# Block-sparse attention and a bilinear FFN on one core: the attention outputs of three batches are turned by a DMA transpose, and the queries lie twice in DRAM

## The chip, the cores and the metric

The kernel runs on one core of a Trainium2 chip. The metric is the time of one execution on the device in microseconds. Before the change three runs gave 824.2, 828.27 and 829.44 us, so the median is 828.27 us.

## The reference

Four batches of eight heads with 768 positions and a head size of 64 go through block-sparse attention (blocks of 32; each block of queries sees its neighbours, the first and the last block, and three sampled ones; the first and the last block see everything). The outputs of all heads of a position make a row x of 512, and 3072 such rows go through (x·w_a)·(x·w_b) and then w_out.

```python
scores = scale * np.matmul(q, k.transpose(0, 1, 3, 2))
mask = np.abs(blk_i - blk_j) <= window
mask = mask | (blk_i == 0) | (blk_j == 0) | (blk_i == n_blocks - 1) | (blk_j == n_blocks - 1)
# ... and the sampled blocks
attn = np.exp(scores - max) / (sum + 1e-09)
x = np.matmul(attn, v)            # (B, H, S, D) -> (B * S, H * D) = (3072, 512)
out = ((x @ w_a) * (x @ w_b)) @ w_out
```

## The kernel before, in words

Values are float32. The kernel takes most operands as a pair of f16 numbers (high and low part), so that a product is the sum of two or three f16 products. The first batch (b = 0) is the exception: its scores and values are multiplied in float32.

**Units.** One block of 32 queries of one batch, all heads, is a unit: 24 units a batch, 96 in all. For a unit TensorE (PE) makes the scores (`s`, line 932, lines 923 and 1068 with it), VectorE (DVE) their maximum, ScalarE (ACT) the exponentials `sm`. ACT and DVE split these in f16 pairs `hl`, a DMA transpose on SyncE's queue (SP) turns them to `pt` (line 1135; line 1239 for the dense first and last unit of a batch), and PE multiplies `pt` with gathered values `VG` into `av` (line 991). SP also issues the gathers of `VG` (lines 706 to 719). They go into two buffers.

**Outputs.** Two units share a bank `av` of PSUM. `output` takes each pair of units: for b > 0 ACT copies one half (`xs`, line 1294), DVE adds the other half (1295) and divides (1296); PE turns the two 128x128 float32 tiles of `xs` with the unit matrix (line 1301, into the same bank), and ACT and DVE split what it wrote in high and low part in `xT` (1312 and 1313). The bank comes free after that. There are 12 pairs in a batch, so 36 in batches two to four.

**FFN.** Eight units (four pairs) make a chunk of 256 rows; there are 12 chunks, and three buffers `xT`. `first_products` makes 12 groups of 24 matmuls for a chunk (line 1350, 128x256 each, `xT` as the moving operand, 3456 in all); `inner` multiplies the two halves; `second_products` makes 12 groups of six for w_out (lines 1432 to 1434), after `split` has made pairs `gh` of the gates.

**Queries of batches two to four.** Half a chunk's queries are loaded on 64 partitions by ACT's queue (line 746); ACT takes the bound (776) and the high part (782), DVE the low part (784); then `turn_queries` copies each part to the other 64 partitions with a DMA on SP (line 822): two for a half, 36 in all. 64 partitions are not enough, because a key's high and low part stand on top of each other on 128 partitions.

**Keys and values.** For each batch four tiles of keys and four of values pass a ring of three buffers `ks`. The bound of a tile of values (`va`, line 581) uses a buffer of that ring for output that nobody reads.

**Order.** The program is written out by a planner. Each flow (a generator) asks for the next instruction with a cost; the planner gives each engine its instructions in an order by estimated times and ranks, and every engine then runs its own queue in that order. A wait at the head of a queue holds up all behind it. `LATE_…` constants are delays that the planner adds to an estimate; they make no instruction wait.

## Time and profile before

| | |
|---|---|
| median of three runs | 828.27 us |
| the profiled execution's own time | 832.1 us |
| its span, first to last instruction | 830.3 us |
| PE busy | 757.6 us, 91% |
| weight loads on PE | 533.0 us, 64% |
| DVE busy | 525.1 us, 63% |
| ACT busy | 485.3 us, 58% |
| POOL (GpSimd) busy | 172.7 us, 21% |
| mean granted clock of PE | 0.971 |
| packets on SP's queue (q1), share of 16 DMA engines | 48.6% |

The durations are those of one execution, whose own time is 3.8 us over the median of the runs. PE is busy in nearly all slices from 150 us to the end; the first 150 us, with the loads and the first batch, leave it idle more often. The durations of matmuls have modelled ends, so for PE the distance from one start to the next says more than the length.

### The profile page before, as it was taken

The page shows a single profiled execution, that of the slowest core. Times are in us where ns is not written, and L with a number is a line of the kernel's source. Part 1 is how long each engine was busy: PE and PEld are TensorE (multiplying, and loading weights), DVE is VectorE, ACT ScalarE, POOL GpSimd, SP SyncE. Part 2 cuts the span into 40 slices and gives each one's busy share as a digit, 9 for nine tenths or more (in the row PEclk, how much of TensorE's full clock was granted, in tenths as well). Part 3 has the DMA queues.
Part 4 walks back from the last instruction along what each step waited for, and adds up shares of the span by engine and source line. Part 5 has one row for each costly group of instructions (what it writes and reads, how often), then busy time and mean ns, then how long its engine had stood idle before and what let it go on. Part 6 is the DMA issues. An engine that isn't in the chain of part 4 may idle for free.

```text
span 830.3 us, 26115 instructions
## 1 busy us (share of the span) xinstructions
PE 757.6 (91%) x10128; PEld 533.0 (64%) x10128; DVE 525.1 (63%) x1495; ACT 485.3 (58%) x1189; POOL 172.7 (21%) x430
## 2 busy tenths in 40 slices
PE   3759699999997989899799999999999999999998
PEld 1426477764586468748558848848758668768853
DVE  3679998866746755686657676766566666532232
ACT  3456777886646554775645666766456655533333
POOL 4405321012123321130223221301123212000000
PEclk9859999999999899999999999999999999999999
DMA  7788877477577688869777779769776665440001
GB/s 226 224 280 252 240 198 213 147 206 176 135 149 144 139 213 148 178 167 185 175 162 137 151 181 228 174 162 188 148 151 148 128 124 128 111 116 2 1 1 52
DMA packets 171803, 130.50 MB, mean 157 GB/s; under 512 B 116894, under 2 KB 138527, under 8 KB 171679
## 3 DMA queue, kind: packets, MB, share of 16 engines
q1 hardware_dynamic: 156844, 86.29, 48.6%
q10 hardware_dynamic: 14832, 42.54, 17.0%
q8 instruction: 80, 1.31, 0.7%
q14 instruction: 47, 0.36, 0.1%
HBM read 86.31 MB, written 11.01 MB: 117 GB/s over the span
## 4 chain that ended last, share of the span: by engine, by line
PE 72%; DMA 10%; DVE 8%; ACT 5%; SPq 2%; issue 2%; ACTq 0%; POOL 0%; POOLq 0%; DVEq 0%
PE ab L1350 40%; PE o L1432 6%; PE o L1434 6%; PE o L1433 6%; PE av L991 5%; PE s L932 4%; DMA VG<-in_v_dram 3%; DMA keysT<-ks 2%; PE av L1301 2%; PE s L923 2%; DMA VG<-vd 2%; ACT gh L1402 1%; DVE gh L1403 1%; PE tp L1039 1%; DMA QZ<-in_q_dram 1%
## 5 line engine op out<-in xcount | busy, mean ns | idle before, releaser
L1350 PE MATMUL ab<-xT,wab 128*128 128x256 f16 x3456 | 396.0, 274 | 2.7 <-DVE g L1368 2.7
L1350 PEld LDWEIGHTS <-wab 128*128 128x128 f16 x3456 | 334.1, 98 | 58.1 <-issue 17.1
L1368 DVE TENSOR_TENSOR g<-g,ab 128x256 f32<-128x256 f32 x144 | 60.4, 419 | 145.8 <-ACT g L1365 141.9
L1365 ACT ACTIVATE g<-ab,f 128x256 f32<-128x256 f32 x144 | 67.9, 471 | 110.5 <-PE ab L1350 106.8
L1402 ACT ACTIVATE gh<-g,scale 128x256 f16<-128x256 f32 x144 | 70.5, 504 | 79.4 <-PE o L1434 74.0
L1403 DVE SCALAR_TENSOR_TENSOR gh<-g,scale,gh 128x256 f16<-128x256 f32 x144 | 68.8, 490 | 75.1 <-ACT gh L1402 73.9
L1432 PE MATMUL o<-wo,gh 128*128 128x512 f16 x288 | 110.4, 383 | 0.1
L1434 PE MATMUL o<-wo,gh 128*128 128x512 f16 x288 | 110.2, 383 | 0.0
L1433 PE MATMUL o<-wo,gh 128*128 128x512 f16 x288 | 110.2, 383 | 0.0
L653 POOL COPY KG<-keysT 128x384 int32<-128x384 int32 (+1 forms) x86 | 47.8, 556 | 278.8 <-PE s L932 237.8
L662 POOL COPY KG<-keysT 128x128 int32 (+1 forms) x264 | 92.6, 388 | 51.8 <-POOL KG L653 32.3
L1095 ACT ACTIVATE sm<-s,low,cq 128x256 f32<-128x256 f32 x132 | 73.7, 560 | 47.4 <-DVE low L1089 38.8
L991 PE MATMUL av<-VG,pt 128*32 128x128 f16 (+2 forms) x3584 | 68.4, 217 | 27.2 <-DMA VG<-in_v_dram 13.0
L421 POOL PARTITION_ALL_REDUCE power<-bound x58 | 22.7, 391 | 296.0 <-DVE bound L1382 126.9
L958 DVE SCALAR_TENSOR_TENSOR hl<-sm,hl 128x256 f16<-128x256 f32 (+1 forms) x156 | 69.6, 450 | 1.7
L1083 DVE TENSOR_REDUCE low<-s 128x2 f32<-128x512 f32 x88 | 60.2, 684 | 13.9 <-PE s L923 9.0
L991 PEld LDWEIGHTS <-pt 128*32 128x32 f16 x2688 | 33.0, 97 | 34.8 <-issue 22.5
L1434 PEld LDWEIGHTS <-gh 128*128 128x128 f16 x288 | 28.4, 99 | 34.6 <-issue 0.8
L1432 PEld LDWEIGHTS <-gh 128*128 128x128 f16 x288 | 28.2, 98 | 34.8 <-issue 4.3
L1433 PEld LDWEIGHTS <-gh 128*128 128x128 f16 x288 | 28.3, 98 | 28.6 <-issue 0.6
L1372 ACT ACTIVATE junk<-g 128x1024 f16<-128x1024 f32 x36 | 38.0, 1055 | 8.5 <-DVE g L1368 8.5
L954 DVE TENSOR_SCALAR hl<-sm 128x256 f16<-128x256 f32 (+1 forms) x125 | 39.3, 317 | 5.5 <-ACT sm L1095 5.2
(122 smaller groups left out, 876.0 us busy)
## 6 DMA issues: line engine op xcount, KB each, us to landing
VG<-vd SPq DMA_DIRECT2D x210, 64.0 KB, 2.2
VG<-vd SPq DMA_DIRECT2D x66, 192.0 KB, 3.2
VG<-vd SPq DMA_DIRECT2D x24, 384.0 KB, 3.8
out_dram<-ou ACTq DMA_DIRECT2D x24, 256.0 KB, 3.5
VG<-in_v_dram SPq DMA_DIRECT2D x74, 64.0 KB, 3.7
stage<-in_v_dram ACTq DMA_DIRECT2D x12, 384.0 KB, 6.7
q<-in_q_dram ACTq DMA_DIRECT2D x18, 256.0 KB, 4.6
vd<-vs SPq DMA_DIRECT2D x12, 384.0 KB, 4.2
```

The source lines that it names most:

```text
L662: nc.gpsimd.tensor_copy(to[:, :, (5 + r) * w : (6 + r) * w], of[:, :, bass.ds(at, w)])
L958: t = yield dve(221 + n * 1.03, lambda: nc.vector.scalar_tensor_tensor(lo, sm, over, hi, ALU.mult, ALU.subtract))
L991: mm(both[hs, :, i % 2, hq] if two else av[hs, i % 2, hq], pt[:, y, hs], of if two or b == 0 else of[:, 0], start=(i % 2 == 0 and hq == 0 ...
L1095: t = yield act(750, lambda hq=hq: nc.scalar.activation(sm[:, hq], ps[:, hq], AF.Exp, bias=low[:, at, hq, 0:1], scale=factor_of(b, cc, hq) ...
L1350: mm(ab[:, i, :], wab[:, f, i, part, kt, :], xc[:, kt, a, :], start=(i == 0 and kt == 0 and part + a == 0), stop=(kt == KT - 1 and a == 1) ...
L1365: yield act(460, lambda: nc.scalar.activation(g, ab[:, 0, :], AF.Copy, scale=f1[:, f : f + 1]))
L1368: t = yield dve(415, lambda: nc.vector.tensor_mul(g, g, ab[:, 1, :]))
L1402: yield act(400, lambda: nc.scalar.activation(gh[:, 0], g, AF.Copy, scale=s))
L1403: t = yield dve(480, lambda: nc.vector.scalar_tensor_tensor(gh[:, 1], g, s, gh[:, 0], ALU.mult, ALU.subtract))
L1432: mm(po, gh[:, 0, js], wo[:, f, 0], start=(f == 0), stop=False)
L1433: mm(po, gh[:, 0, js], wo[:, f, 1], start=False, stop=False)
L1434: mm(po, gh[:, 1, js], wo[:, f, 0], start=False, stop=(f == NF - 1))
```

## The change

The outputs of batches two to four are no longer turned by PE. After line 1296 ACT makes the high part `xo` of `xs`, DVE the low part, and one DMA transpose on SP turns the four 128x128 f16 tiles (high and low of two tiles) straight into `xT`. The bank `av` is free in the plan after the addition. So that a transpose writes one piece, `xT` is laid out by pairs: pair, high or low, tile, four groups of heads, 32 positions. The products of line 1350 read 256 columns of it as eight runs of 32. The first batch keeps PE's transposes, into the new layout.

The queries are laid out twice, one below the other, in DRAM; a load brings both copies to 128 partitions, ACT and DVE split on all of them, and the copies of `turn_queries` are gone. The ring `ks` has two buffers; `va` writes to `junk`, a tile that only ACT writes.

```diff
-KS_BUFS = 3
+KS_BUFS = 2
+XO_BUFS = 2
+LATE_XO = 1000
+LATE_XT = 2500
...
-    xT = [kvp.tile([P, KT, 2, CH], F16, name=f"xT{i}") for i in range(X_BUFS)]
+    xT = [kvp.tile([P, PER // 2, 2, 2, KT, BLK], F16, name=f"xT{i}") for i in range(X_BUFS)]
...
-        done = yield from take("ks", KS_BUFS)
-        spare = work.tile([P, 2 * NT, P], F16, tag="ks", name=f"va{b}_{g}", bufs=KS_BUFS)
         end = yield act(1020, lambda: nc.scalar.activation(
-            spare[:, :NT], t, AF.Abs,
-            accum_out=bound_v[:, b * NG + g : b * NG + g + 1],
-        ))
-        done.fire(end)
+            junk.rearrange("p f c -> p (f c)")[:, : NT * P].rearrange("p (t x) -> p t x", t=NT),
+            t, AF.Abs, accum_out=bound_v[:, b * NG + g : b * NG + g + 1],
+        ))
...
-            end = yield load_way(700, lambda t=t, half=half: nc.scalar.dma_start(
-                t[:D], q[b, c, :, half * NG : (half + 1) * NG]
+            end = yield load_way(2000, lambda t=t, half=half: nc.scalar.dma_start(
+                t, q[b, c, :, half * NG : (half + 1) * NG]
...
-    def turn_queries(cc, half, a):
-
-        heads = slice(half * NG, (half + 1) * NG)
-        yield SPARE
-        end = yield sp(650, 400, lambda: nc.sync.dma_start(
-            QT[cc][D:, 1 - a, heads], QT[cc][:D, a, heads]
-        ))
-        q_ready[cc].fire(end)
...
-        to = xT[p % X_BUFS][:, :, :, i % PER * BLK : (i % PER + 2) * BLK]
+        to = xT[p % X_BUFS][:, i % PER // 2]
...
             yield act(470, lambda: nc.scalar.copy(xs, sums[:, 1]))
-            yield dve(418, lambda: nc.vector.tensor_add(xs, xs, sums[:, 0]))
+            t = yield dve(418, lambda: nc.vector.tensor_add(xs, xs, sums[:, 0]))
+            read.fire(t + LATE_AV)
             yield dve(430, lambda: nc.vector.tensor_mul(xs, xs, over))
-        ps = bank[:, 1].rearrange("p (g i x) -> p g i x", g=NG, i=2)
+            gone = yield from take("xo", XO_BUFS)
+            xo = work.tile([P, 2, 2, P], F16, tag="xo", name=f"xo{b}_{i}", bufs=XO_BUFS)
+            flat = xs.rearrange("p i a d -> p i (a d)")
+            yield act(400, lambda: nc.scalar.copy(xo[:, 0], flat))
+            t = yield dve(420, lambda: nc.vector.tensor_sub(xo[:, 1], flat, xo[:, 0]))
+            held.fire(t)
+            t = yield sp(900, 760, lambda: nc.sync.dma_start_transpose(
+                to.rearrange("p a x k q -> p (a x) (k q)"), xo.rearrange("p a i c -> p (a i c)")
+            ))
+            gone.fire(t + LATE_XO)
+            x_ready[cc].fire(t + LATE_XT)
+            x_ready[cc].fire(t + LATE_XT)
+            return
...
                                 mm(
-                                    ab[:, i, :], wab[:, f, i, part, kt, :], xc[:, kt, a, :],
+                                    ab[:, i, :].rearrange("p (j x q) -> p j x q", j=PER // 2, x=2),
+                                    wab[:, f, i, part, kt, :], xc[:, :, a, :, kt, :],
...
+        a = np.concatenate([a, a], axis=2)
```

Three places show how the instructions move. In the names below a number behind a tile counts pieces or allocations.

PE before, at the fourth pair of the second batch (`av_6`, `xs_6`), between two groups of second products (`o`, `gh`):

```order
L1433 MATMUL o_1_4589<-wo,gh_0_4557 128x512
L1434 LDWEIGHTS gh_0_4557
L1434 MATMUL o_1_4589<-wo,gh_0_4557 128x512
L1301 MATMUL av_6_4329<-eye,xs_6_4553 128x4x32 x2
L1432 LDWEIGHTS gh_1_4558
L1432 MATMUL o_0_4588<-wo,gh_1_4558 128x512
```

In the changed kernel no row of line 1301 is left on PE behind the first batch, 12 instead of 48 pairs in all; the groups stand next to each other there.

ACT before, at the same pair, from the copy of `xs_6` to the high part in `xT`:

```order
L1294 COPY xs_6_4553<-av_6_4329 128x256
L951 ACTIVATE hl_4517<-sm_4504 128x256
L1402 ACTIVATE gh_3_4624<-g_0_3241,scale 128x256
L776 ACTIVATE QT_4198,bound<-q_1_4506 64x1024
L1095 ACTIVATE sm_4636,den<-s_4554,low,cq 128x256
L1402 ACTIVATE gh_4_4647<-g_4_3694,scale 128x256
L1312 ACTIVATE xT_86<-av_6_4329 128x4x64
```

ACT in the changed kernel, at the same pair: `xo_6` is the high part of `xs_6`, and `ab_11` the last group of first products of the chunk before this pair's own:

```order
L749 DMA q_1_4442<-in_q_dram 128x1024
L1286 COPY xs_6_4486<-av_6_4281 128x256
L1087 ACTIVATE sm_4563,den<-s_4419,low,cq 128x256
L1087 ACTIVATE sm_4565,den<-s_4487,low,cq 128x256
L1373 ACTIVATE g_8_4259<-ab_11_4382,f_99 128x256
L1293 CAST xo_6_4581<-xs_6_4486 128x256
```

The high part now reads `xs` instead of what PE wrote, and its place is behind the copy of `ab_11`, a result of PE. On PE, behind the pair's last `av` rows, one unit's scores, that last group (`ab_11`), one unit's `av` rows and one more unit's scores lie ahead of `ab_0` of the pair's own chunk, the first group that reads this chunk's `xT`.

SP before, while the third batch's last keys (`keysT`) are turned, with copies of queries (`QT`) and the semaphores of each row:

```order
L1135 DMA_TRANSPOSE pt_5849<-hl_5769 128x8x128 [waits DMAHW4_49,DVE_49]
L560 DMA_TRANSPOSE keysT_76<-ks_3_5535 128x12x128 [waits DMAHW6_49,DVE_49]
L1135 DMA_TRANSPOSE pt_6122<-hl_6018 128x8x128 [waits DMAHW7_49,DVE_49]
L822 DMA QT_5237<-QT_5237 64x1024 [waits DMAHW0_49,Activation_49]
L822 DMA QT_5237<-QT_5237 64x1024 [waits DMAHW1_49]
L1135 DMA_TRANSPOSE pt_6179<-hl_6133 128x8x128 [waits DMAHW2_49,DVE_49]
L714 DMA VG_85<-vd_79 96x1024 [waits DMAHW3_49,PE_49]
```

SP in the changed kernel, at the same pair as ACT above:

```order
L722 ISA
L722 DMA VG_84<-vd_79 32x1024 [waits DMAHW2_49]
L722 ISA
L722 DMA VG_84<-vd_79 32x1024 [waits DMAHW3_49]
L1296 DMA_TRANSPOSE xT_86<-xo_6_4581 128x4x128 [waits DMAHW4_49,DVE_49]
L717 DMA VG_85<-vd_79 96x1024 [waits DMAHW5_49,PE_49]
L626 TENSOR_LOAD offs
```

The two copies of `QT` are gone from the queue, and a transpose of `xo` stands behind one unit's gather into `VG_84` and ahead of the next into `VG_85`, with a wait for DVE.

## Rows read from the trace of the kernel before

**Rows 1.** Busy time per stretch: length, each engine's busy us, PEclk, DMA share, GB/s.

```profile
200.00:300.00 100.00, 93.15 (x1312) 60.84 (x1311) 65.68 (x190) 57.61 (x145) 25.73 (x70) 0.97 0.70 151
300.00:450.00 150.00, 136.74 (x1962) 98.29 (x1960) 93.73 (x276) 88.16 (x213) 33.35 (x80) 0.98 0.80 173
450.00:760.00 310.00, 304.24 (x4275) 221.15 (x4274) 193.15 (x564) 179.16 (x442) 59.15 (x157) 1.00 0.68 146
```

**Rows 2.** PE groups by shape, 236 to 760 us: busy, mean, idle before, releasers.

```profile
L991 PE MATMUL av<-VG,pt 128*32 128x128 f16 x1296 | 42.1, 224 | 10.5 <-DMA VG<-vd 5.9 <-DMA pt<-hl 4.5
...
L1301 PE MATMUL av<-eye,xs 128*128 128x128 f32 x72 | 14.8, 287 | 13.7 <-DVE xs L1296 8.5 <-ACT gh L1402 4.5 <-DVE low L1089 0.4
```

**Rows 3.** PE in order of time, 455 to 459 us: start, length, what.

```profile
457.10 0.38 PE L1301 MATMUL av<-eye,xs 128*128 128x128 f32 x2
457.32 1.91 PE L1350 MATMUL ab<-xT,wab 128*128 128x256 f16 x16
```

**Rows 4.** PE in order of time, 238 to 244.4 us.

```profile
239.48 0.61 PE L932 MATMUL s<-KG,QT 128*32 128x256 f16 x16
240.02 2.79 PE L1350 MATMUL ab<-xT,wab 128*128 128x256 f16 x24
242.75 0.53 PE L991 MATMUL av<-VG,pt 128*32 128x128 f16 x32
243.20 0.44 PE L1301 MATMUL av<-eye,xs 128*128 128x128 f32 x2
243.57 0.27 PE L1068 MATMUL s<-mrows,ident 128*32 128x192 bf16 x4
```

**Rows 5.** PE in order of time, 405 to 409.4 us; brackets: idle before, releaser.

```profile
406.66 0.41 PE L1301 MATMUL av<-eye,xs 128*128 128x128 f32 x2 [4.16 <-ACT gh L1402]
...
407.45 0.61 PE L1432 MATMUL o<-wo,gh 128*128 128x512 f16 x1
407.85 0.63 PE L1433 MATMUL o<-wo,gh 128*128 128x512 f16 x1
```

**Rows 6.** ACT and DVE groups by shape, 236 to 760 us.

```profile
L1296 DVE TENSOR_TENSOR xs<-xs,den 128x256 f32<-128x256 f32 x36 | 15.9, 441 | 0.4
...
L1313 DVE SCALAR_TENSOR_TENSOR xT<-av,xT 128x256 f16<-128x256 f32 x36 | 15.0, 418 | 1.9 <-ACT xT L1312 1.8
L1295 DVE TENSOR_TENSOR xs<-xs,av 128x256 f32<-128x256 f32 x36 | 14.9, 413 | 1.9 <-ACT xs L1294 1.7
...
L1312 ACT ACTIVATE xT<-av 128x256 f16<-128x256 f32 x36 | 13.5, 375 | 3.9 <-PE av L1301 3.9
...
L1294 ACT COPY xs<-av 128x256 f32<-128x256 f32 x36 | 13.0, 361 | 1.0 <-PE av L991 0.9
...
L951 ACT ACTIVATE hl<-sm 128x256 f16<-128x256 f32 x28 | 11.4, 408 | 0.0
```

**Rows 7.** SP's transposes of eight blocks, line 1135: hold ns min/median/max; landing.

```profile
L1135 SPq DMA_TRANSPOSE pt<-hl x66: 1231/1274/2644, 231.2 to 716.6; - x66
...
DMA to landing us min/median/max: 3.0/3.7/5.7
```

**Rows 8.** SP's copies of the queries, line 822: the same.

```profile
L822 SPq DMA_DIRECT2D QT<-QT x36: 467/546/1271, 165.9 to 654.3; - x36
...
DMA to landing us min/median/max: 2.2/4.1/6.0
```

**Rows 9.** What SP's queue waited for: total us, times, longest.

```profile
SPq L714 <- PE av L991: 73.5, 31, 13.3
SPq L706 <- PE av L991: 50.2, 24, 5.9
```

**Rows 10.** PE in order of time, 401.2 to 402.6 us.

```profile
401.29 0.44 PE L991 MATMUL av<-VG,pt 128*32 128x128 f16 x24
401.56 0.26 PE L1068 MATMUL s<-mrows,ident 128*32 128x192 bf16 x4
401.64 0.61 PE L932 MATMUL s<-KG,QT 128*32 128x256 f16 x16
```

More of the change, by code (lines that the diff above doesn't have):

```diff
@@ L46 @@
 LATE = 16
+LATE_X = 800
+LATE_X0 = 0
 RIDE = 24
@@ L296 @@
     B, NCH, D, H, CH = q.shape
+    D //= 2
     NF, P, DM = w_a.shape
@@ L384 @@
     v_stored = [Event(NG) for _ in range(B)]
-    q_ready = [Event(3 if cc < NCH else 5) for cc in range(NC)]
+    q_ready = [Event(3) for _ in range(NC)]
     tables = Event()
@@ L774, in half_queries @@
         heads = slice(half * NG, (half + 1) * NG)
-        high, low_ = QT[cc][:D, 0, heads], QT[cc][:D, 1, heads]
+        high, low_ = QT[cc][:, 0, heads], QT[cc][:, 1, heads]
         yield act(1230, lambda: nc.scalar.activation(
-            high, t[:D], AF.Abs, accum_out=bound[:D, at : at + 1]
+            high, t, AF.Abs, accum_out=bound[:, at : at + 1]
         ))
@@ L780, in half_queries @@
         known.fire(end)
-        s = scale[:D, at : at + 1]
-        end = yield act(1120, lambda: nc.scalar.activation(high, t[:D], AF.Copy, scale=s))
-        plan.start(turn_queries(cc, half, 0), u0 - LEAD_Q, end)
+        s = scale[:, at : at + 1]
+        yield act(1120, lambda: nc.scalar.activation(high, t, AF.Copy, scale=s))
         end = yield dve(1250, lambda: nc.vector.scalar_tensor_tensor(
-            low_, t[:D], s, high, ALU.mult, ALU.subtract
+            low_, t, s, high, ALU.mult, ALU.subtract
         ))
         freed.fire(end)
-        plan.start(turn_queries(cc, half, 1), u0 - LEAD_Q, end)
+        q_ready[cc].fire(end)
     def next_queries(cc):
@@ L812, in plain_queries @@
             end = yield sp(650, 700, lambda y=y: nc.sync.dma_start(
-                t[parts_of[y], y], q[0, cc, :, y * NG : (y + 1) * NG]
+                t[parts_of[y], y], q[0, cc, parts_of[y], y * NG : (y + 1) * NG]
             ))
@@ L1294, in output @@
             yield act(470, lambda: nc.scalar.copy(xs, sums[:, 1]))
-            yield dve(418, lambda: nc.vector.tensor_add(xs, xs, sums[:, 0]))
+            t = yield dve(418, lambda: nc.vector.tensor_add(xs, xs, sums[:, 0]))
+            read.fire(t + LATE_AV)
             yield dve(430, lambda: nc.vector.tensor_mul(xs, xs, over))
-        ps = bank[:, 1].rearrange("p (g i x) -> p g i x", g=NG, i=2)
+            gone = yield from take("xo", XO_BUFS)
[11 more added lines that the diff above has]
+            return
+        ps = bank[:, 1].rearrange("p (i c) -> p i c", i=2)
+        yield LATE_X if b else LATE_X0
         def turns_():
@@ L1301, in turns_ @@
                 nc.tensor.transpose(
-                    ps[:, :, x], xs[:, x].rearrange("p a d -> p (a d)"), eye
+                    ps[:, x], xs[:, x].rearrange("p a d -> p (a d)"), eye
                 )
@@ L1309, in output @@
         s = scale[:, at_v : at_v + 1] if b == 0 else 1.0
-        of = ps.rearrange("p g i x -> p g (i x)")
-        hi, lo = to[:, :, 0], to[:, :, 1]
+        of = ps.rearrange("p i c -> p (i c)")
+        hi, lo = (to[:, a].rearrange("p x k q -> p (x k q)") for a in range(2))
         yield act(470, lambda: nc.scalar.activation(hi, of, AF.Copy, scale=s))
```

## The prediction

> **What bounds the kernel now.** I read the busy time per stretch first [rows 1]. From 200 us on PE is the engine that the rest feeds: 93.15 of 100 us, 136.74 of 150, 304.24 of 310, while DVE stays under 66% and ACT under 60% in the same stretches. Its idle time there is 6.85 + 13.26 + 5.76 = 25.9 us, and the granted clock is 0.97, 0.98 and 1.00, so most of these stretches runs at 2.4 GHz. What PE has to do, and what it waits for, is the time.
>
> Next, PE's groups by shape from 236 to 760 us [rows 2]. The 72 transposes of batches two to four (line 1301) are credited with 14.8 us, and PE stood idle for 13.7 us just ahead of them: 8.5 for `xs` of DVE, 4.5 for ACT. The only other large waits are 10.5 us ahead of the `av` products (line 991), all for DMA. So over half of PE's idle time in the steady part stands in front of the instructions that the change removes, because they sit in PE's queue at a fixed place and hold up products that need nothing from them.
>
> **The change, part by part.** *PE's transposes.* The lengths have modelled ends, so I take distances of starts. Between two product groups, a pair starts at 457.10 and the next group at 457.32: 0.22 us [rows 3]. Behind `av` products the pair starts at 243.20 and the next instruction at 243.57: 0.37 us [rows 4]. These are the least and the most where PE doesn't wait; 36 pairs make 7.9 to 13.3 us. Pairs of the shorter kind are more frequent: 0.28 us each, 10 us. This is full gain as long as PE is the bound.
>
> *The waits ahead of them.* At most 13.7 us come back. The longest, 4.16 us at 406.66, will mostly stay: the second products behind it start at 407.45 [rows 5] and need `gh`, which ACT (line 1402) only makes in that moment; the releaser named is that very line. That leaves 9.5 us. In the others DVE was late with `xs` while products further down the queue had their operands. But products that come earlier also reach their own limits (`gh`, gathers) earlier. I take 8 us, bounds 0 and 13.7.
>
> *ACT and DVE.* Both keep their count: line 1312's 375 ns becomes a conversion like line 951's (408), line 1313's 418 ns a subtraction of the same length class as 1295's 413 [rows 6]. That is 36 x 33 ns = 1.2 us on ACT, which has 40% free: nothing. The splits of the queries work on 128 partitions instead of 64, with the same number of elements on each: nothing; the cover is the lead of several units with which they run. `va` no longer waits for a buffer, and the ring shrinks from three to two for fewer users: nothing either way, with the waits for it hidden under products.
>
> *The way to the next chunk.* The transposes of PE were short; the new path is longer. Before: 0.4 us on PE, then 375 and 418 ns. Now: 408 and about 418 ns, then a DMA transpose, whose eight-block relatives land 3.0 us (minimum) to 3.7 us (median) after issue [rows 6, 7]. A pair's rows of x come some 3 us later. In the new order nearly every chunk has 12 us or more of other PE work between the last `av` and the first product that reads them, so it stays hidden. One does not: the first chunk of the second batch. Behind its last `av` PE has one unit's scores (0.54 us, 239.48 to 240.02), one group of first products (2.7 us, 240.02 to 242.75), `av` (0.45 us, 242.75 to 243.20) and scores again [rows 4]: 4.3 us. In the same time ACT must copy `xs` (361), DVE add (413) and divide (441), and ACT can convert only behind its reading of that last group's result, so not before 3.3 us; then come 408 and 418 ns [rows 6], and 3.0 us on DMA. That is 7.1 us against 4.3. I take 3 us of new idle time; bounds 0 (PE waits there for the next unit's `pt` anyway) and 6 (the transpose waits in SP's queue and lands late, at up to 5.7 us [rows 7]).
>
> *SP and DMA.* SP loses 36 copies of the queries at 546 ns (20 us) and gains 36 transposes. An eight-block one holds the queue for 1274 ns [rows 7, 8]; four blocks hold it for between half of that and all of it: 23 to 46 us. So SP is between 3 and 26 us busier, over more than 500 us. What hides this: SP itself waited 73.5 + 50.2 us for PE to free buffers of `VG` [rows 9]. On the 16 DMA engines come 36 x 4 blocks to the program's 816 of before (66 x 8, 24 x 6 and 12 x 12), 18% more; the copies of QT go, and the loads of queries double. The share was 0.68 to 0.80 [rows 1], so transfers will take somewhat longer. The cost shows as waits ahead of `av`, 10.5 us so far: I take +1 us, bounds -1 and +4 (a tenth less to 40% more).
>
> *The products' read pattern.* 256 columns now come as eight runs of 32 f16 instead of one. No instruction of before reads its moving operand in just this way. The nearest rows: half of `av`'s products read two runs of 64, and 24 of them (12 of 128 columns, 12 of 64) go in four column tiles from 401.29 to 401.56, 0.27 us, where 576 columns at 2.4 GHz take 0.24; the next four, 192 columns each with repeated elements, take 0.08 us to the next start, which is 192 / 2.4 [rows 10]. A pattern of several levels costs nothing there. I take 0; bounds 0 and the price in the third rival.
>
> *First batch.* Its order on PE is nearly the same, and the first 200 us with their loads aren't touched: 0.
>
> Sum on the profiled execution's own 832.1 us: -10 - 8 + 3 + 1 = 818 us. That execution was 3.8 us over the median of the runs, so the forecast for the median is **814 us**, 1.7% less.
>
> **The rivals.** *All waits vanish.* If the 13.7 us go in full, the transposes cost 0.30 us a pair and the fourth chunk's longer way is hidden by the wait for `pt`: 832.1 - 11 - 13.7 - 3.8 = 804 us. For it: nothing that PE waits for in front of line 1301 is needed by the products behind it. Against it: 4.16 us belong to `gh` [rows 5].
>
> *The waits move.* PE finds the same idle time in front of other instructions, as in a queue whose pace the attention sets: every unit still goes through ACT, DVE, SP and a DMA. Then only the removed work counts, and part of that is refilled: -10 + 3 + 4 = -3, or 825 us. For it: PE's 25.9 us of idle time lie where few products are ready to fill in; against it: from 450 to 760 us PE is at 98% [rows 1], so there the pace is PE's own.
>
> *The read pattern costs.* If every run but the first costs a column time more at 2.4 GHz (0.42 ns), a product takes 2.9 ns longer: 3456 x 2.9 = 10 us, 824 us. From 4 ns a product on, the gain of 14 us is gone. Against it stand rows 10, so I leave this rival little. The Trainium skill, Advanced Engine Details and Errata, section Memory Cachelines, has SBUF reads at full speed where each 16-byte line is hit at least twice; runs of 32 f16 hit each line eight times, so by it this rival would cost nothing, and no row of before shows it for runs as short as these.
>
> *SP's queue becomes the bound, and the kernel gets slower.* Each transpose of `xo` waits for DVE at the head of SP's queue, and the next gather into `VG` stands behind it. What PE waited for directly (8.5 us on `xs`) then reaches it by way of SP, with the landing of a gather on top. Its place is the 36 pairs in batches two to four; its price is the 26 us of longer holds (upper bound above) plus 8.5 us, less what SP's slack swallows. If three quarters of these 34 us reach PE: 814 + 26 = 840 us. It decides from 14 us on. For it: SP's `pt` transposes and gathers already end 10.5 us of PE's waits. Against it: 124 us of SP's own waits for PE. The Trainium skill, VectorE: DVE Perf Modes, section The three transpose paths, gives 390 ns for a 128x128 bf16 transpose on TensorE and 1309 ns by DMA, and its Rules for kernel authors advise TensorE where PSUM will do; as a price for each block (an estimate from that page) 144 blocks would hold SP for 188 us, and the change would lose by far more. The trace doesn't agree with that as a price in a queue: eight blocks hold it for 1.27 us [rows 7].
>
> **How the numbers follow.** Forecast 0.52, all waits vanish 0.14, waits move 0.18, read pattern 0.07, SP bound 0.09. The range leaves out the last and a part of the read pattern's: from 800 (every bound on the good side: 832.1 - 13.3 - 13.7 - 1 - 3.8 = 800.3) to 830 (on the other side 832.1 - 8 + 6 + 4 - 3.8 = 830.3). The runs of before lie within 0.6% of each other, and about 1% is what a measurement here can tell from no change: under 820 is faster, over 836.5 slower. Faster: 0.14 and nearly all of 0.52, 0.64. Slower: the SP case and a tail of the read pattern, 0.12. Same: 0.24.
>
> **What the profile after would show.** PE without line 1301 behind 236 us, and less idle time: some 15 to 18 us instead of 25.9 from 200 to 760 us, with a wait of 2 to 5 us ahead of the first group of the fourth chunk's products. A group of 24 products that still takes 2.7 us from start to start. SP's transposes of four blocks held under 1.27 us. I am wrong if waits ahead of `av` grow by over 10 us (SP or DMA), if products take longer, or if idle time only changes its place.

## Result and profile after

The changed kernel takes **841.6 us**, the median of four runs (835.42 to 848.05), beside 828.86 us for the kernel before on the same chip: a ratio of **1.0138** [1.0094, 1.0182]. The ratio is taken from the executions that the chip did not slow down, so it is not the quotient of the two medians. I forecast 814 us, faster, with a range up to 830; it is slower and lies outside.

The profiled execution of the changed kernel took 835.4 us and is the lowest of its four runs; that of before, 832.1, was above its median. So the two traces show 3.3 of the 12.7 us between the medians; they say where time goes, and the medians of the experiments say how much.

| us, profiled execution | before | after |
|---|---|---|
| span | 830.3 | 833.6 |
| PE busy | 757.6 | 749.5 |
| rest of the span | 72.7 | 84.1 |

PE works 8.1 us less and stands idle 11.4 us more. In the changed kernel the scores are at line 924, `av` at 983, the first products at 1357, the second at 1440 to 1442, the transpose of `xo` at 1296 and the eight-block transpose of `pt` at 1127.

Busy time per stretch of the changed kernel, columns as in [rows 1]:

```profile
200.00:300.00 100.00, 90.82 (x1274) 58.79 (x1272) 65.95 (x195) 60.12 (x151) 23.48 (x64) 0.97 0.71 153
300.00:450.00 150.00, 139.79 (x2003) 100.41 (x2004) 91.92 (x263) 89.08 (x218) 30.23 (x82) 0.97 0.82 180
450.00:760.00 310.00, 295.66 (x4160) 212.12 (x4158) 186.88 (x550) 179.86 (x448) 56.03 (x154) 0.99 0.72 153
```

PE's idle time in these stretches is 9.2 + 10.2 + 14.3 = 33.7 us, where it was 25.9 [rows 1]. The net growth is all from 450 us on, 14.3 us in place of 5.8: just where I had read "the pace is PE's own".

PE's groups by shape from 236 to 760 us, the same view as [rows 2]:

```profile
L1357 PE MATMUL ab<-xT,wab 128*128 128x256 f16 x2481 | 286.7, 276 | 5.9 <-DVE g L1376 3.6 <-DMA xT<-xo 2.3
L1440 PE MATMUL o<-wo,gh 128*128 128x512 f16 x192 | 74.5, 388 | 7.7 <-ACT gh L1410 7.7
...
L983 PE MATMUL av<-VG,pt 128*32 128x128 f16 x1276 | 41.4, 224 | 17.2 <-DMA pt<-hl 8.7 <-DMA VG<-vd 5.3 <-DMA q<-in_q_dram 3.3
```

The 13.7 us in front of the transposes are gone with them. In their place stand 7.7 us ahead of the second products, 5.9 ahead of the first, and 17.2 ahead of `av`, which were 10.5 [rows 2]. Over half of the 7.7 is the wait for `gh` that I had said would stay; it stood in front of a transpose before and stands in front of line 1440 now:

```profile
403.39 0.61 PE L1440 MATMUL o<-wo,gh 128*128 128x512 f16 x1 [4.04 <-ACT gh L1410]
```

Two of the other places can be followed.

The chain of waits of the changed kernel between 250 and 280 us (start, length, what):

```profile
249.93 2.73 PE ab L1357 x24
...
265.97 3.21 DMA VG<-vd
269.19 0.40 ACT xo L1293
...
271.07 4.02 DMA xT<-xo
275.14 4.62 PE ab L1357 x24
```

PE itself in order of time, from the scores behind the last `av` of this pair on (brackets: idle before, releaser):

```profile
265.44 0.61 PE L924 MATMUL s<-KG,QT 128*32 128x256 f16 x16
...
271.58 0.44 PE L983 MATMUL av<-VG,pt 128*32 128x128 f16 x24 [2.60 <-DMA VG<-vd]
...
275.14 4.62 PE L1357 MATMUL ab<-xT,wab 128*128 128x256 f16 x24 [2.30 <-DMA xT<-xo]
```

This is the fourth chunk. The transpose of `xo` takes 4.02 us from its issue to the product that waits for it, and PE stands idle for 2.30 us there, beside the +3 of the forecast. The way itself is longer than I had reckoned, 265.44 to 275.14, 9.7 us in place of 7.1; PE's wait of 2.60 us for `VG` just before hid as much of it. The 24 products at 249.93 take 2.73 us to the next instruction, as before (240.02 to 242.75 [rows 4]).

SP's queue in order of time, 623 to 637 us (start, length, line, what), and under it PE (brackets: idle before, releaser):

```profile
625.23 2.19 SPq L1296 DMA_TRANSPOSE xT<-xo  x1
627.51 0.53 SPq L717 DMA_DIRECT2D VG<-vd  x1
629.01 1.40 SPq L722 DMA_DIRECT2D VG<-vd  x3
630.52 1.36 SPq L1127 DMA_TRANSPOSE pt<-hl  x1
```

```profile
630.18 2.79 PE L1357 MATMUL ab<-xT,wab 128*128 128x256 f16 x24
635.12 0.56 PE L983 MATMUL av<-VG,pt 128*32 128x128 f16 x32 [2.15 <-DMA pt<-hl]
```

A transpose of `xo` holds the queue for 2.19 us, the longest of all 36; a unit's gathers and then its `pt` follow one behind the other, and `av` waits 2.15 us for that `pt`. DVE had made the last part of `hl` that can belong to it by 628.21, 2.3 us ahead of the issue at 630.52:

```profile
627.78 0.43 DVE L950 SCALAR_TENSOR_TENSOR hl<-sm,hl 128x256 f16<-128x256 f32 x1
```

By these rows the hold reaches PE here nearly in full. The 3.3 us put down to `q` in the groups above are a single wait at 565.13. The transposes themselves, in the view of [rows 7]: hold in ns (minimum, median, maximum), those of `xo` (four blocks) first, then six blocks and eight blocks:

```profile
L1296 SPq DMA_TRANSPOSE xT<-xo x36: 1190/1218/2190, 242.2 to 757.9; - x36
```

```profile
L1231 SPq DMA_TRANSPOSE pt<-hl x24: 1211/1218/2504, 204.2 to 743.6; - x24
```

```profile
L1127 SPq DMA_TRANSPOSE pt<-hl x66: 1232/1257/3656, 222.5 to 725.4; - x66
```

Four blocks hold SP nearly as long as eight. I had put them between half of 1274 ns and all of it. Over all 36 the hold adds up to 47.6 us, since some are held longer than the median. And what SP's queue waited for (total, times, longest):

```profile
SPq L717 <- PE av L983: 45.3, 23, 8.2
SPq L709 <- PE av L983: 39.0, 14, 6.7
...
SPq L1296 <- DVE xo L1294: 21.6, 5, 11.8
```

SP's spare time ahead of the gathers falls from 123.7 us [rows 9] to 84.3.

### The profile page after: what moved, and what is told of

Read it like the earlier page. It is cut to its first block, busy times and chain, and to the rows that moved or that the text cites. A ratio compares the mean times of both kernels' runs of the same rounds, so it can differ in the third digit from the quotient of the medians.

```text
span 833.6 us, 25988 instructions
## 1 busy us (share of the span) xinstructions
PE 749.5 (90%) x10056; PEld 524.7 (63%) x10056; DVE 518.6 (62%) x1477; ACT 490.4 (59%) x1207; POOL 169.5 (20%) x430
## 4 chain that ended last, share of the span: by engine, by line
PE 66%; DMA 16%; ACT 6%; DVE 6%; SPq 2%; issue 2%; ACTq 0%; POOL 0%; DVEq 0%
PE ab L1357 35%; PE o L1440 7%; PE o L1442 7%; PE o L1441 7%; PE av L983 5%; DMA pt<-hl 5%; PE s L924 3%; DMA VG<-in_v_dram 2%; DMA QZ<-in_q_dram 2%; DMA stage<-in_v_dram 1%; DMA VG<-vd 1%; ACT sm L1087 1%; PE s L915 1%; DMA keysT<-in_k_dram 1%; DMA keysT<-ks 1%
## 5 line engine op out<-in xcount | busy, mean ns | idle before, releaser
L665 POOL COPY KG<-keysT 128x128 int32 (+1 forms) x264 | 89.0, 374 | 48.1 <-POOL KG L656 28.7
L924 PE MATMUL s<-KG,QT 128*32 128x256 f16 x1056 | 40.7, 274 | 0.0
```

Source lines behind the costliest of these rows:

```text
L665: nc.gpsimd.tensor_copy(to[:, :, (5 + r) * w : (6 + r) * w], of[:, :, bass.ds(at, w)])
L924: mm(to[h * BLK : (h + 1) * BLK], q_block(cc, i, 4 * hq + h, a), rhs(4 * hq + h), start=(first and a == 0), stop=(a == 1), skip_group_chec ...
```

## Experiments

Three theories went in. **A**: the 36 transposes of `xo` on SP and on the DMA engines lengthen the way of `pt` and of the gathers. **B**: the planner, given other flows, writes another order on every queue, and in it PE's waits lie elsewhere; the transposes cost little. **C**: products that read eight runs of 32 are slower. Ratios are to the kernel before, run on the same chip (the experiments ran on three), with 95% intervals. Where I subtract two ratios, the interval is the root of the sum of both squares; 0.01 is 8.3 us.

**One part at a time.** *e1_layout*: the kernel before with the new layout of `xT` alone; every queue keeps its order.

```diff
-    xT = [kvp.tile([P, KT, 2, CH], F16, ...
+    xT = [kvp.tile([P, PER // 2, 2, 2, KT, BLK], F16, ...
-    ab[:, i, :], wab[:, f, i, part, kt, :], xc[:, kt, a, :],
+    ab[:, i, :].rearrange(...), wab[:, f, i, part, kt, :], xc[:, :, a, :, kt, :],
```

> The kernel before with the new layout of xT alone: products read eight runs of 32 columns, PE still turns all 48 pairs, and every queue has the same instructions in the same order as before. Theory A (added DMA work on SP and the 16 DMA engines lengthens the way of pt) and theory B (the planner's new order moves the waits) both expect the time of before, 829 within 4 us, and groups of 24 products at 109 ns a product. Theory C (the read pattern costs) expects 837 us or more and products at 112 ns or more.

829.5 us, 1.0006 [0.9962, 1.005]. C is refuted.

*e2_ring*: the kernel before with the ring of two.

```diff
-KS_BUFS = 3
+KS_BUFS = 2
-            spare[:, :NT], t, AF.Abs,
+            junk.rearrange(...)[:, : NT * P]..., t, AF.Abs,
```

> The kernel before with two buffers in the ring ks and the bound of the values written to junk; queries, layout and PE's transposes as before. No DMA work is added, but the planner writes another order. Theory A expects 829 within 4 us. Theory B, by which a new order with the same work moves PE's waits, expects a difference of 4 us or more in either direction, with waits ahead of other lines.

833.9 us, 1.0056 [1.0021, 1.0091]. I had put the ring at nothing; with the order that follows from it, it costs about 5 us (2 to 8 by the interval).

*e3_queries*: the kernel before with queries twice, split on 128 partitions, no copies on SP.

```diff
-    def turn_queries(cc, half, a):
-...
-            end = yield load_way(700, lambda ...: nc.scalar.dma_start(t[:D], q[...]
+            end = yield load_way(2000, lambda ...: nc.scalar.dma_start(t, q[...]
```

> The kernel before with the queries twice in DRAM, split on 128 partitions, without the 36 copies on SP; ring of three, layout and PE's transposes as before. Theory A expects SP's 20 us of copies and their traffic (4.7 MB) to go and the loads to double (4.7 MB more): 829 within 4 us, pt landing as before. If it is the double loads that harm, 835 us or more with waits of PE behind a load of q. Theory B: a difference of either sign, with the order.

840.7 us, 1.0163 [1.011, 1.0215]. A change that takes 36 DMAs from SP and adds none there loses as much as the whole. A kernel can become as slow as this without the transposes.

*e4_turn*: ring and layout, `x` turned by DMA, queries as before.

```diff
+            xo = work.tile([P, 2, 2, P], F16, tag="xo", ...
+            t = yield sp(900, 760, lambda: nc.sync.dma_start_transpose(...
```

> The kernel before with the outputs of batches two to four turned by DMA, the new layout, the ring of two and junk; the queries as before, with their 36 copies on SP. It has the transposes on SP and no relief from the copies, so theory A expects the worst of all: 845 us or more, pt landing over 4.0 us in the median, waits ahead of av over 20 us. Theory B expects it anywhere between 815 and 845, without pt landing later. If PE's gain of some 10 us and the waits ahead of line 1301 come back, 814.

837.3 us, 1.0115 [1.0064, 1.0166]. The waits ahead of `av` from 200 us on:

```profile
L991 PE MATMUL av<-VG,pt 128*32 128x128 f16 x1344 | 44.0, 224 | 19.8 <-DMA pt<-hl 16.4 <-DMA VG<-vd 3.3
```

Slower too, as B allows. A had expected the worst of all, 845 us or more, with `pt` landing over 4.0 us after issue in the median (it is 3.8); that is a miss.

**Order or work.** *e5_plan_only*: the kernel before, and of the changed kernel nothing but one number, an estimate of the planner. The work is the same (two of the conversions to `hl` go to ACT in place of DVE); the order isn't.

```diff
-            end = yield load_way(700, lambda t=t, half=half: nc.scalar.dma_start(
+            end = yield load_way(2000, lambda t=t, half=half: nc.scalar.dma_start(
```

> The kernel before with a single number of the planner changed: its estimate of the transfer of a half of the queries, 2000 ns instead of 700. No instruction, size or byte differs, only the order in the queues. Theory B (a new order moves PE's waits) expects a time away from 829 by 4 us or more, slower rather than faster. Theory A (added DMA work) expects 829 within 4 us.

835.3 us, 1.0124 [1.0042, 1.0205]. PE from 200 us on, groups by shape:

```profile
L991 PE MATMUL av<-VG,pt 128*32 128x128 f16 x1344 | 43.8, 224 | 10.2 <-DMA pt<-hl 6.7 <-DMA VG<-vd 3.5
L1301 PE MATMUL av<-eye,xs 128*128 128x128 f32 x74 | 15.5, 291 | 17.9 <-DVE xs L1296 12.7 <-ACT gh L1402 3.5 <-DVE low L1089 1.6
```

An order alone costs 10 us (3 to 17 by the interval, from three runs), with 17.9 us of waits ahead of PE's transposes where [rows 2] have 13.7; this trace is of the longest of the three runs. B is a mechanism of this kernel.

*e6_queries_700* is e3 with the estimate left at 700.

```diff
-            end = yield load_way(2000, ...
+            end = yield load_way(700, ...
```

> The queries twice in DRAM, split on 128 partitions, no copies on SP, as in the run on the queries before, but with the planner's old estimate of 700 ns for a load. Theory A with the double loads as its cause expects 838 to 843 as there. Theory B expects another time than 840.7, nearer to 829, since the order is another one again.

844.4 us, 1.0216 [1.0127, 1.0305]. The estimate as such is not what made e3 slow. B had expected a time nearer to 829, and missed.

*e7_double_loads*: the exact order of before, each load of queries brings both copies, the second is not used.

```diff
-                t[:D], q[b, c, :, half * NG : (half + 1) * NG]
+                t, q[b, c, :, half * NG : (half + 1) * NG]
```

> The kernel before in exactly its own order on every engine, but each load of queries brings both copies to 128 partitions (4.7 MB more, read by nobody: the splits and the copies on SP stay as before). Theory A, with the loads as cause, expects 835 us or more and waits of PE behind them. Theory B expects 829 within 4 us.

829.7 us, 1.0027 [0.9983, 1.007]. The doubled loads cost nothing that can be measured. The splits on 128 partitions take as long as those on 64 did (1142 ns on ACT for a high part in e3 and before), so in e3 and e6 the order is left, by exclusion; no run keeps their work in the order of before.

*e8_dummy_turns*: the order of e2_ring, and behind 36 of the `pt` transposes a second one of four blocks of `hl` into a tile that nobody reads.

```diff
+            if pd is not None:
+                nc.sync.dma_start_transpose(pd, hl[:, 0].rearrange("p h k -> p (h k)"))
```

> The kernel with the ring of two (833.9 us) in exactly its order on PE, and behind the transpose of every second sparse unit's hl on SP one more transpose of four blocks of hl into a tile that nobody reads: 36 in all, as many as the change adds, and unknown to the planner. Theory A expects 842 us or more (waits ahead of av over 15 us). Theory B expects 834 within 4 us.

854.4 us, 1.0274 [1.0164, 1.0383], 0.0218 ± 0.0115 over e2. So A is a mechanism too, in an order that leaves no place for the transposes. But the time isn't where A had looked for it, over 15 us ahead of `av`:

```profile
L988 PE MATMUL av<-VG,pt 128*32 128x128 f16 x1344 | 43.2, 223 | 9.9 <-DMA pt<-hl 9.7
```

In the trace of e2 these waits are 6.9 us. The dummies also keep `hl` longer, so the 20 us are no clean price.

**The price of the transposes in the changed kernel.** *e9_no_turn*: its own order on PE, without the 36 DMAs (so `x` isn't turned).

```diff
-            yield act(400, lambda: nc.scalar.copy(xo[:, 0], flat))
+            yield act(400, lambda: nc.scalar.copy(tf[:, 0], flat))    # tf is xT
-            t = yield sp(900, 760, lambda: nc.sync.dma_start_transpose(...
+            t = yield sp(900, 760, lambda: None)
```

> The changed kernel in exactly its own order on TensorE, without the 36 DMA transposes of xo: ScalarE's cast and VectorE's subtraction write straight into xT, so the activations are not turned and the result of the products is not the reference's; everything else is left as it is. Theory A (the 36 transposes on SP's queue and the DMA engines lengthen the way of the softmax's transposes): the kernel falls to about 820 us, below the kernel before, since TensorE's work is 10 us less and the waits that the transposes made are gone. Theory B (the planner's other order moves TensorE's waits, the transposes themselves cost little): about 838 to 842 us, as the changed kernel (841.6). Between 827 and 836 both have a share, and the difference from 841.6 is the share of the transposes.

828.2 us, 1.0007 [0.9968, 1.0047]. Between both forecasts: the transposes cost 0.0131 ± 0.0059, 11 us by the ratios (13 by the medians), and without them the kernel is still no faster than before. PE from 200 us on:

```profile
L1355 PE MATMUL ab<-xT,wab 128*128 128x256 f16 x2880 | 327.7, 274 | 2.1 <-DVE g L1374 2.1
L1438 PE MATMUL o<-wo,gh 128*128 128x512 f16 x274 | 105.5, 385 | 8.9 <-ACT gh L1408 7.7 <-ACT ou L1454 1.2
...
L983 PE MATMUL av<-VG,pt 128*32 128x128 f16 x1344 | 44.2, 226 | 12.4 <-DMA pt<-hl 10.1 <-DMA VG<-vd 2.1
```

Its PE is busy 748.3 us, 9.3 less than before: the removed work, as forecast. But its idle time from 200 to 760 us is no less than before, 25.3 us to 25.9: in place of the 13.7 us in front of line 1301 there are waits for `gh` (7.7, ahead of the second products) and for `pt`. Two more traces have the order of before on PE, DVE and SP, those of *e1_layout* and *e7_double_loads*; their executions took 827.4 and 825.3 us, that of e9 825.8. The stretch from 200 to 760 us in e1, e7 and e9 (columns as in [rows 1]):

```profile
200.00:760.00 560.00, 540.14 (x7591) 384.57 (x7590) 353.54 (x1031) 326.85 (x803) 120.39 (x308) 0.98 0.72 154
```

```profile
200.00:760.00 560.00, 537.97 (x7574) 385.06 (x7572) 352.35 (x1030) 326.75 (x802) 116.17 (x301) 0.99 0.72 161
```

```profile
200.00:760.00 560.00, 534.73 (x7530) 380.04 (x7528) 346.70 (x1013) 332.89 (x822) 112.46 (x304) 0.98 0.67 152
```

PE is idle for 19.9 and 22.0 us in the order of before and for 25.3 in e9. Over the whole span it is idle for 68.8, 68.9 and 75.7 us, and busy for 756.9, 754.6 and 748.3: the removed work came back as waits. SP's spare time here is

```profile
SPq L717 <- PE av L983: 75.8, 36, 8.4
SPq L709 <- PE av L983: 40.4, 15, 6.1
```

116.2 us; with the transposes it is 84.3, and PE's idle time goes to 33.7. By what PE waits for, that growth is not in `pt`, for which `av` waits 10.1 us here and 8.7 in the changed kernel; it is in `VG` (2.1 to 5.3), in the wait put down to `q` (3.3), in `xT` (2.3) and in `g` (2.1 to 3.6).

*e10_exchange*: the order of e2_ring, PE's pairs taken out, the casts in their old places, and the 36 transposes on SP without the planner's knowledge.

```diff
-        t = yield pe(280, turns_)
+        t = yield pe(280, turns_ if b == 0 else (lambda: None))
+                nc.vector.tensor_sub(xo[:, 1], flat, xo[:, 0])
+                nc.sync.dma_start_transpose(to..., xo...)
```

> The order of e2_ring (833.85 us) on every engine, with the 36 pairs of TensorE transposes of batches two to four taken out of TensorE's queue, the casts left in their places, now out of xs into xo, and the 36 DMA transposes issued on SP at the places where the casts stood, without the planner knowing of them. Theory B: with the order kept, the exchange itself gives back what the pairs cost TensorE, 10 us of work and some of the waits ahead of them: 818 to 828 us. Theory A: the transposes delay those of the softmax's outputs and the gathers behind them on SP: 840 us or more.

855.9 us, 1.032 [1.0234, 1.0405]. PE from 200 us on:

```profile
L1360 PE MATMUL ab<-xT,wab 128*128 128x256 f16 x2880 | 333.6, 276 | 12.3 <-DMA xT<-xo 7.2 <-DVE g L1379 4.6 <-ACT xT L1310 0.3
...
L988 PE MATMUL av<-VG,pt 128*32 128x128 f16 x1344 | 44.5, 227 | 36.7 <-DMA pt<-hl 34.9 <-DMA VG<-vd 1.6
```

B's forecast fails: kept in an order that is good for something else, the exchange loses 0.026 over e2, nearly all ahead of `av`, for `pt`.

*e11_after_xt1500* and *e12_after_q700*: the changed kernel with one estimate of the planner changed each.

```diff
-LATE_XT = 2500
+LATE_XT = 1500
```

> The changed kernel with one number of the planner changed, its estimate of the time from the cast of xo to the turned xT (2500 before, 1500 here): the same work and the same instructions in another order. Theory B: another order is another draw, several us from 841.6 on either side, 828 to 850 us. Theory A: the same transposes on the same queue, so 838 to 845 us.

842.3 us, 1.0168 [1.0116, 1.022]; both theories allow it.

```diff
-            end = yield load_way(2000, ...
+            end = yield load_way(700, ...
```

> The changed kernel with the planner's estimate of the way of a load of queries put back to 700 from 2000, which is the number that the kernel before has: the same work and instructions as the changed kernel, in another order. Theory B: another draw, several us from 841.6 on either side, 828 to 850 us. Theory A: 838 to 845 us, as the changed kernel.

834.9 us, 1.0047 [0.9994, 1.0099]. The same work in three orders: 842.3, 841.6 and 834.9 us. Only e12 differs from the changed kernel by more than the noise, by 0.0091 ± 0.0069; every engine has the same instructions in both.

**What of a transpose costs.** *e13_copies*: the changed kernel's own order, plain copies in place of the transposes (so `x` isn't turned).

```diff
-            t = yield sp(900, 760, lambda: nc.sync.dma_start_transpose(
+            t = yield sp(900, 760, lambda: nc.sync.dma_start(
```

> The changed kernel in exactly its own order, with each of the 36 DMA transposes of xo replaced by a plain DMA copy of xo into xT on the same queue at the same place: the same bytes and the same waits, but not turned, so the products' result is not the reference's. In the trace of the changed kernel a transpose of xo holds SP 1.32 us and a copy between DRAM and SBUF 0.4 to 0.56. If the holding of SP's queue (or the transposes' own way through the DMA engines) costs the 13 us, this falls to 828 to 833 us; if another DMA on the queue, its waits for ScalarE and VectorE or its bytes cost them, it stays at 838 to 843 us.

834.4 us, 1.0049 [1.0008, 1.009]. SP's hold:

```profile
L1296 SPq DMA_DIRECT2D xT<-xo x36: 475/499/1430, 246.9 to 757.4; - x36
```

*e14_half_as_many*: one transpose of eight blocks for two pairs, PE's order unchanged.

```diff
-            xo = work.tile([P, 2, 2, P], F16, tag="xo", ..., bufs=XO_BUFS)
+            xo = both[:, i // 2 % 2]         # both: [P, 2, 2, 2, P], one buffer
-            t = yield sp(900, 760, lambda: nc.sync.dma_start_transpose(to..., xo...))
+            t = yield sp(900, 760, (lambda: nc.sync.dma_start_transpose(pair..., both...))
+                if last else (lambda: None))
```

> The changed kernel in its own order on TensorE, with 18 transposes of eight blocks in place of 36 of four: one for two pairs, issued at the place of the second pair's. The same blocks and bytes are turned. A transpose holds SP about 1.3 us whatever its size in the traces (1.32 with four blocks, 1.40 with six and with eight). If the time that SP is held decides: half of the 13 us comes back, 834 to 837 us. If the blocks and bytes decide: 840 to 843 us. Against both stands that the first pair of two is turned later, for which the products may wait: up to 3 us for a chunk.

833.5 us, 1.0034 [0.9998, 1.007].

```profile
L1305 SPq DMA_TRANSPOSE xT<-xo x18: 1232/1272/2197, 248.0 to 763.2; - x18
```

| in the changed kernel's order | hold of SP in all, us | over e9 |
|---|---|---|
| 36 transposes of four blocks | 47.6 | 0.0131 ± 0.0059 |
| 18 transposes of eight, the same blocks | 25.4 | 0.0027 ± 0.0053 |
| 36 copies, the same bytes | 19.6 | 0.0042 ± 0.0057 |

The price goes down with the time that SP's queue is held, not with the blocks or the bytes: e14 lies 0.0104 ± 0.0057 under the changed kernel, e13 0.0089 ± 0.0060. That it is in proportion isn't shown, as both small prices could be nothing or half. e14 turns as many blocks on the DMA engines as the changed kernel does, so their work alone isn't the price.

*e15_q700_no_turn*: the order of e12 without transposes.

```diff
-            end = yield load_way(2000, ...     # in e9_no_turn
+            end = yield load_way(700, ...
```

> The order of e12_after_q700 (834.9 us), without the 36 transposes, ScalarE and VectorE writing straight into xT, as in e9_no_turn: not turned, so the result is not the reference's. The price of the transposes in a second order: if it is a price of the transposes as such, about 13 us, so 820 to 824 us; if it hangs on what the order puts beside them, less, 826 to 834 us.

818.5 us, 0.9866 [0.9805, 0.9927]. The transposes cost 0.0181 ± 0.0080 here. Without them, in this order the removal of PE's pairs is seen as a gain.

*e16_real_times*: the changed kernel, planned with holds near the measured ones.

```diff
-            t = yield sp(900, 760, ...        # xo, four blocks
+            t = yield sp(1330, 1000, ...
-            t = yield sp(1100, 1130, ...      # pt, six
+            t = yield sp(1400, 1130, ...
-        t = yield sp(1300, 1500, ...          # pt, eight
+        t = yield sp(1400, 1500, ...
```

> The changed kernel with the planner's three estimates of how long a transpose holds SP set near what the trace shows (four blocks 900 to 1330 ns, six 1100 to 1400, eight 1300 to 1400): the same instructions in another order. If the changed kernel is slow because its order is written with too cheap transposes, 826 to 836 us. If an order's time is a draw that the estimates do not steer, 828 to 850 us with no direction.

827.0 us, 0.9979 [0.9944, 1.0013]: as fast as before, and 0.0159 ± 0.0056 under the changed kernel with all its instructions.

*e17_real_times_no_turn*: this order without transposes.

```diff
-            t = yield sp(1330, 1000, lambda: nc.sync.dma_start_transpose(...
+            t = yield sp(1330, 1000, lambda: None)
```

> The order of e16_real_times (827.0 us) on TensorE, without the 36 transposes, ScalarE and VectorE writing straight into xT: not turned, so the result is not the reference's. In the two orders written with 900 ns for a transpose the 36 cost 13.4 and 16.3 us. If their price is the same in any order, about 811 to 815 us here. If it is smaller in an order that knows how long they hold SP, 818 to 826 us.

822.2 us, 0.9898 [0.9858, 0.9939]. The transposes cost 0.0081 ± 0.0053. PE from 200 us on, e16 first:

```profile
L1440 PE MATMUL o<-wo,gh 128*128 128x512 f16 x276 | 106.8, 387 | 6.2 <-ACT gh L1410 4.9 <-ACT ou L1456 1.2
...
L983 PE MATMUL av<-VG,pt 128*32 128x128 f16 x1344 | 44.4, 225 | 18.6 <-DMA VG<-vd 12.6 <-DMA pt<-hl 5.8
```

```profile
L1438 PE MATMUL o<-wo,gh 128*128 128x512 f16 x276 | 106.0, 384 | 6.8 <-ACT gh L1408 5.5 <-ACT ou L1454 1.2
...
L983 PE MATMUL av<-VG,pt 128*32 128x128 f16 x1344 | 43.8, 224 | 12.3 <-DMA VG<-vd 10.1 <-DMA pt<-hl 2.0
```

Here, in these two traces, the transposes add some 6 us ahead of `av`. Two thirds of what e16 gains lie in the order without the transposes (1.0007 to 0.9898), a third in cheaper transposes; the three prices, 0.0131, 0.0181 and 0.0081, overlap in their intervals, so that they are cheaper there isn't shown.

*e18_half_real_times*: 18 transposes, known to the planner with 1400 ns.

```diff
+            if not last:
+                held_x[m] = gone
+                return
-            t = yield sp(900, 760, ...
+            t = yield sp(1400, 1500, lambda: nc.sync.dma_start_transpose(pair..., both...))
```

> One transpose of eight blocks for two pairs, 18 in all, and the planner knows them: 1400 ns on SP each, as for the other transposes. If SP's held time sets the price of the exchange, this is the fastest form that turns the activations: 815 to 826 us, below the kernel before (829.5) and the changed one. If an order's time is mostly a draw, 820 to 845 us.

838.5 us, 1.0116 [1.0066, 1.0166]. The waits ahead of `av`:

```profile
L984 PE MATMUL av<-VG,pt 128*32 128x128 f16 x1344 | 44.2, 226 | 19.2 <-DMA pt<-hl 12.1 <-DMA VG<-vd 6.9 <-issue 0.2
```

A miss: the form with the shorter hold, in an order written for it, is slower than in e14. A planner that knows the holds better doesn't reliably write a better order. No kernel here that turns `x` by DMA is faster than the kernel before by more than the noise.

## Why the prediction was wrong

In short, two terms of the sum failed. The waits that I counted as gained (8 us) came back in front of other instructions in the new order, with all of the removed work. And the transposes on SP's queue, which I took to be hidden, cost some 11 us where I had set 3 + 1 aside.

**PE's work: right, at the low end.** 10 us forecast, bounds 7.9 and 13.3. PE is 9.3 us less busy in e9 and 8.1 in the changed kernel than in the trace of before, and e9 8.6 and 6.3 less than e1 and e7.

**The read pattern, the loads, the fourth chunk: right.** 0 for the pattern (e1, 1.0006), nothing for the queries' loads (e7, 1.0027), 2.3 us for the way to the next chunk where I took 3. That the last comes so near is luck: the way took 9.7 us, not 7.1, and a wait for `VG` hid the rest. Nor is it shown that the 2.3 us came on top, for without the transposes (e9) PE waits at the next `av` instead:

```profile
278.17 0.83 PE L983 MATMUL av<-VG,pt 128*32 128x128 f16 x32 [3.16 <-DMA pt<-hl]
```

**"I take 8 us" of the waits: the first step that failed.** The waits in front of the removed instructions did go, but PE found as many elsewhere: from 200 to 760 us 25.9 us of idle time before, and 19.9 and 22.0 in two more traces of that order, against 25.3 in e9, which has the changed kernel's order and no transposes. The part that I kept back, 4.16 us for `gh`, did stay (4.04). For the rest I reasoned that products further down the queue had their operands, as if the rest of the queue stayed where it was; the removal, the ring and the queries made the planner write every queue anew, and `gh` and `pt` came late instead. This is the rival that the waits move, which I gave 0.18, and the last sign of being wrong that I named. How much of this belongs to the ring (0.0056 in another order, e2) and how much to the rest of the order isn't separated. That an order alone is worth this much is shown by e5 (1.0124), by e12 against the changed kernel, and by e15 and e17 against e9: without transposes, the same work takes 0.9866, 0.9898 and 1.0007.

**"SP and DMA: I take +1 us", bounds -1 and +4: the second step that failed.** The transposes cost 0.0131 ± 0.0059, some 11 us; the longer way to the next chunk is in that price, so it stands against 3 + 1. The hold came out at the upper end of what I had put: four blocks hold SP nearly as long as eight (1218 and 1257 ns), 47.6 us in all, against 21.4 of the copies before, so 26 us more. What failed is the cover. I set the hold against SP's own waits for PE (124 us) as if these could swallow it. 84.3 us of those waits are still there in the changed kernel, and PE pays all the same: they lie where the buffers of `VG` are full, while a transpose can come where SP is already passing a unit's gathers and `pt` one behind the other, and there (625 to 637 us above) it goes to PE nearly in full. That the price falls when the hold does is shown by e13 and e14. By which waits most of it reaches PE isn't: that stretch is one place, and over the whole trace the growth over e9 lies with `VG`, `q`, `xT` and `g`.

The rival of SP's queue, to which I gave 0.09, had this mechanism, and its 840 us lie beside the 841.6. The number is luck: it put 26 us on top of a gain of 14, where the runs show no gain and 11 us. The waits for DVE at the head of the queue, one of its two causes, are not most of it, as the copies of e13 wait for the same operands in the same places. The 26 us are nearly met in an order that makes no room (e10: 0.026 over e2, 22 us, although PE has 10 us less to do, so the transposes with their later casts cost over 30 us there).

The Trainium skill, VectorE: DVE Perf Modes, section The three transpose paths, gives 1309 ns for one 128x128 bf16 transpose by DMA. The hold of an instruction here has that size (1218 to 1257 ns), but for four, six or eight f16 blocks alike, and e14 shows that halving the number of instructions, not of blocks, gives most of the time back.

**The sum.** Without its transposes the changed kernel is at the time before (1.0007): what 6 to 9 us of removed work gave, the order took back. The transposes then add 11 to 13 us, and that is the whole of the loss of 12.7. Two rivals came true together; I had priced each alone. The cause of the 1% that the orders differ by was followed only to the instructions that PE waits for; which rule of the planner makes one order better stays open.

## What to carry to other kernels

In a kernel whose queues are written by a planner, an edit is two edits: the work, and a new order of everything; price the order at the spread of neighbouring orders (here over 1% either way) before counting waits as gained, and run the new order without the new work to tell them apart. Up to eight blocks, a DMA transpose here cost its queue the same whatever its size: price it by count and by what stands behind it, batch it (e14), and look for the places where the queue runs without a gap instead of adding up its idle time. A batched form planned anew can still lose what it gained (e18). Idle time in front of an instruction is no gain of its removal until the next instruction's operands are shown to be there in the order that will be run.

## What the runs showed of the hardware

In the changed kernel a DMA transpose of 128-row f16 tiles holds SP's queue 1218 ns for four blocks, 1218 for six and 1257 for eight (medians), and lands 3.4, 2.8 and 4.1 us after issue; a plain copy of the four blocks' bytes holds it 499 ns (e13) and lands after 3.5. Loads of queries of twice the bytes on 128 in place of 64 partitions leave the time as it was (1.0027 [0.9983, 1.007]).
